# A banded-attention and two-MLP kernel on one core: q and k come transposed, values and weights in blocks, masks from memory

## The chip, the core and the metric

The kernel runs on one core of one Trainium2 chip. Five engines work side by side: PE (matrix products, with its own weight loads), DVE (elementwise work and reductions), ACT (activation functions and copies), POOL (elementwise work; it also issues some transfers) and SP, which here only issues transfers between memory and the chip. Each engine takes its instructions strictly in their written order and waits on semaphores. The metric is the device time of one execution in microseconds, as the median of three runs. Work that the host does before the launch, such as a new layout of the inputs, is not in it.

## What is computed

```python
# q, k, v: (4, 8, 576, 64); heads 0-3 see a plain window, heads 4-7 a dilated one
scores = scale * np.matmul(q, k.transpose(0, 1, 3, 2))
mask_plain = (rel >= 0) & (rel < 32)
mask_dil = (rel >= 0) & (rel < 128) & (rel % 4 == 0)
scores = np.where(masks, scores, -1e9)
attn = softmax(scores); x = attn @ v            # then x: (2304, 512)
h = np.maximum(np.maximum(x @ w1, x @ w2), x @ w3); x = h @ w_out      # d_ff 768
h = x @ w_in                                                          # d_ff 2048
P = a[0] + a[1]*h + a[2]*h**2 + a[3]*h**3
Q = 1 + abs(b[0])*abs(h) + abs(b[1])*h**2
out = (P / (Q + 1e-6)) @ w_out
```

Weights of the MLPs come as 64-bit floats.

## The kernel before, in words

Tokens are cut into 12 chunks of 192 (three to a batch entry), and two chunks make a unit of 384 tokens; there are six units. The attention of a chunk is written as steps, each for group p (the plain heads) and group d (the dilated ones): T transposes the raw rows of k or q on PE (four products with an identity matrix, L265) and copies the result into kTp, kTd (ACT, L274) or into both halves of a block-diagonal qTp, qTd (DVE L278 and ACT L279); S makes the scores (L308 adds the mask as a product for chunks 0 to 3, L317 the score products); MX the row maxima (L334, L337); E the exponentials (L345); SB the division (L355 to L357); X the transpose of the attention weights (L370, with copies L372 or L374); V the product with v (L390, L396); VE the split of the result into two parts x1h and x1l (L411, L412).

The order of this work is written by hand. START lists what comes before the first MLP: chunks 0 and 1, some loads, the first steps of the weight conversion, and W:n, n products of zeros that keep PE busy (L663). UNIT0 and UNIT list the steps of the next unit's two chunks, row by row beside the product groups of the running unit's first MLP. Within this, a scheduler places each instruction on its engine, and it may pull a step of unit 1 up into the end of START.

The weights of the first MLP (18 pieces for the three maxout matrices, 6 for the output matrix) are loaded as 64-bit words and converted on chip. Per piece: an ACT step (L480), three DVE steps on integers (L490, L493, L496), a copy on ACT (L510) and a subtraction on POOL (L518). The three products of every MLP term (L535 to L537) use the two parts. The 32 pieces of the second MLP are converted beside units 1 to 4 and come back from memory later.

The stages in time are: START (up to the first product of L535), unit 0 with the conversion of the first MLP's weights, units 1 to 5 of the first MLP (units 1 to 4 carry the attention of chunks 4 to 11), and the second MLP.

qTp, qTd, kTp and kTd have one buffer each. The raw q and k rows are loaded in pieces of 96 KB, two to a step, six steps ahead. The masks, the identity matrix and the zeros of qTp and qTd are made on chip by POOL and DVE.

Of the kernel before, what the change touches and what calls it, by code (L numbers as in the profile page):

```python
# [17 lines left out]
LN2 = 0.6931471805599453  # L18
# [12 lines left out]
START = """  # L31
# [8 lines left out]
Ta:p,k Ta:p,q Sa:p  # L40
Ta:d,k Ta:d,q MXa:p Ea:p SBa:p
# [7 lines left out]
Va:d Tb:p,k  # L49
VEa:d  # L50
Tb:p,q
Tb:d,k Sb:p
MXb:p Tb:d,q Eb:p
# [11 lines left out]
Ta:p,k  # L65
Ta:p,q Ta:d,k Sa:p Ta:d,q
# [7 lines left out]
Tb:p,k Va:d Tb:p,q  # L74
VEa:d
-
Sb:p Tb:d,k VEa:p
-
-
Tb:d,q MXb:p  # L80
# [10 lines left out]
def kernel(  # L91
    ctx: ExitStack,
    tc: tile.TileContext,
    q: bass.AP,
    k: bass.AP,
    v: bass.AP,
    w1: bass.AP,
    w2: bass.AP,
    w3: bass.AP,
# [8 lines left out]
    B, H, S, D = q.shape  # L108
    NT, DM = out.shape
    FF1 = w1.shape[1]  # L110
    FF2 = w_in2.shape[1]
# [4 lines left out]
    CH = 192  # L116
# [13 lines left out]
    NEG = -1.0e9 / SCALE  # L130
# [9 lines left out]
    T_MM = 2  # L140
    QK = 6
# [43 lines left out]
    # The queries of two heads (or of two residues of a head) stand on the diagonal of one  # L185
    # stationary operand, their keys one above the other in the moving one.
# [4 lines left out]
    qk_seq = [(c, g, nm) for c in range(NCH) for g in ("p", "d") for nm in ("k", "q")]  # L191
    qk_n = [0]

    def load_qk(n):
        while qk_n[0] < min(n, len(qk_seq)):
            c, g, nm = qk_seq[qk_n[0]]
            qk_n[0] += 1
            b, ci = divmod(c, NC)
            src = q if nm == "q" else k
            t0 = CH * ci  # L200
            t = at.tile([2 * M, 2, 4 * D], F32, tag="qk", bufs=QK, name="qk")
            for i in range(2):
                if g == "p":
                    nc.sync.dma_start(
                        out=t[:, i, :].rearrange("p (h d) -> p h d", h=NP),
                        in_=src[b, 0:NP, t0 + 96 * i:t0 + 96 * i + 96, :].rearrange(
                            "h p d -> p h d"))
                else:
                    nc.sync.dma_start(
                        out=t[M * i:M * i + M],  # L210
                        in_=src[b, NP + 2 * i:NP + 2 * i + 2, t0:t0 + CH, :].rearrange(
                            "g (m r) d -> m g (r d)", r=4))
            at_raw[c, g, nm] = t
# [8 lines left out]
    def load_v(c):  # L222
        b, ci = divmod(c, NC)
        vp = at.tile([WP, BP, NP, D], F32, tag="vp", name=f"vp{c}")
        for i in range(BP):
            k0 = key0(ci, i)
            nc.sync.dma_start(
                out=vp[:, i], in_=v[b, 0:NP, k0:k0 + WP, :].rearrange("h p d -> p h d"))
        m0, nm = dil(ci)
# [221 lines left out]
    def cols(w, f):  # L451
        return w[:, 128 * f:128 * f + 128].rearrange("(c p) f -> p c f", p=128)
# [443 lines left out]
```

## Time and profile before

| | us |
|---|---|
| median of 3 runs | 856.75 |
| lowest and highest run | 853.81, 858.59 |
| span of the profiled execution | 857.5 |
| PE busy in that span | 828.7 (97%) |
| DVE busy | 660.1 (77%) |
| ACT busy | 510.7 (60%) |
| POOL busy | 138.6 (16%) |

The span runs from the first to the last instruction of one profiled execution; no other time of that execution is given, and it lies 0.75 us above the median of the runs. Busy shares are means over stages with different limits, and on PE a busy stretch also counts products that run at half the clock.

### The profile page before, as it was taken

What the parts mean: (1) busy time and instruction counts of PE and PEld (TensorE: products, weight loads), DVE (VectorE), ACT (ScalarE), POOL (GpSimd) and SP (SyncE); (2) the same over time, 40 slices, a digit from 0 to 9 for tenths busy, and PEclk for the clock granted to TensorE, in tenths of its full rate; (3) what the DMA queues carried; (4) which work ended last, traced back from release to release, by engine and by line L of the source; (5) the groups of instructions that cost most, each with busy time, mean ns of one, the idle gap of its engine ahead of it and who ended that gap; (6) DMA issues with size and microseconds to landing.
All of it is one profiled execution on the core that took longest, in us unless ns stands there. A gap on an engine that the chain in (4) does not pass through costs nothing.

```text
span 857.5 us, 13838 instructions
## 1 busy us (share of the span) xinstructions
PE 828.7 (97%) x5167; PEld 764.3 (89%) x5167; DVE 660.1 (77%) x1200; ACT 510.7 (60%) x1071; POOL 138.6 (16%) x172
## 2 busy tenths in 40 slices
PE   8997889999999999999998999999999999999997
PEld 6686779999999999999997889999999999999996
DVE  4699956657666756753529899999999999999996
ACT  4575733334333434424548788778778778777775
POOL 3155451120011011104952000000000000000000
PEclk9699999999999999999998999999999999999999
DMA  8675423645646545415740002002002001000100
GB/s 193 167 230 166 142 57 108 176 139 170 180 138 183 166 148 163 137 49 189 223 128 20 1 1 74 1 1 74 1 0 75 1 1 37 2 0 1 38 1 37
DMA packets 77474, 77.57 MB, mean 90 GB/s; under 512 B 37536, under 2 KB 65952, under 8 KB 77408
## 3 DMA queue, kind: packets, MB, share of 16 engines
q1 hardware_dynamic: 72112, 59.66, 24.8%
q0 software_dynamic: 5296, 17.04, 5.4%
q8 instruction: 40, 0.66, 0.3%
q14 instruction: 26, 0.21, 0.1%
HBM read 58.85 MB, written 17.83 MB: 89 GB/s over the span
## 4 chain that ended last, share of the span: by engine, by line
PE 83%; DVE 8%; issue 3%; ACT 3%; DMA 2%; SPq 1%; POOL 0%; ACTq 0%; DVEq 0%
PE mm L537 10%; PE mm L536 10%; PE mm L535 10%; PE acc L832 8%; PE acc L831 8%; PE acc L830 8%; PE h L535 8%; PE h L536 8%; PE h L537 8%; PE sc L317 3%; DVE cvt L496 2%; DVE cvt L493 2%; PE tpp L370 2%; DMA raw<-in_moe_w_in_dram 1%; PE tpq L265 1%
## 5 line engine op out<-in xcount | busy, mean ns | idle before, releaser
L535 PE MATMUL mm<-x1h,w1s 128*128 128x384 f32 x432 | 149.9, 347 | 0.0
L537 PE MATMUL mm<-x1h,w1s 128*128 128x384 f32 x432 | 146.5, 339 | 2.5 <-POOL w1s L518 2.5
L536 PE MATMUL mm<-x1l,w1s 128*128 128x384 f32 x432 | 146.3, 339 | 0.9 <-DVE x1l L412 0.9
L535 PE MATMUL h<-x2h,w2s 128*128 128x384 f32 x384 | 130.9, 341 | 3.8 <-DVE p L791 3.8
L536 PE MATMUL h<-x2l,w2s 128*128 128x384 f32 x384 | 130.5, 340 | 0.0
L537 PE MATMUL h<-x2h,w2s 128*128 128x384 f32 x384 | 130.4, 340 | 0.0
L831 PE MATMUL acc<-w2s,gh 128*128 128x512 f32 x288 | 113.5, 394 | 0.0
L830 PE MATMUL acc<-w2s,gh 128*128 128x512 f32 x288 | 113.2, 393 | 0.0
L832 PE MATMUL acc<-w2s,gl 128*128 128x512 f32 x288 | 110.3, 395 | 0.0
L781 ACT ACTIVATE q<-h 128x384 f32<-128x384 f32 x96 | 47.3, 493 | 80.1 <-PE h L537 79.0
L788 DVE SCALAR_TENSOR_TENSOR q<-q,cs,ab 128x384 f32<-128x384 f32 x96 | 67.7, 705 | 30.3 <-ACT ab L782 30.3
L537 PEld LDWEIGHTS mm<-x1h,w1s 128*128 128x128 f32 x432 | 81.6, 189 | 4.0 <-POOL w1s L518 4.0
L536 PEld LDWEIGHTS mm<-x1l,w1s 128*128 128x128 f32 x432 | 81.9, 190 | 2.2 <-DVE x1l L412 2.2
L535 PEld LDWEIGHTS mm<-x1h,w1s 128*128 128x128 f32 x432 | 81.8, 190 | 0.4
L535 PEld LDWEIGHTS h<-x2h,w2s 128*128 128x128 f32 x384 | 73.0, 190 | 8.2 <-DVE p L791 4.1
L536 PEld LDWEIGHTS h<-x2l,w2s 128*128 128x128 f32 x384 | 73.1, 190 | 3.8
L537 PEld LDWEIGHTS h<-x2h,w2s 128*128 128x128 f32 x384 | 72.9, 190 | 0.3
L554 DVE TENSOR_TENSOR m<-mm,m 128x384 f32<-128x384 f32 x72 | 39.7, 552 | 41.5 <-PE mm L537 23.3
L783 ACT ACTIVATE p<-h,cs 128x384 f32<-128x384 f32 x96 | 65.0, 678 | 0.0
L832 PEld LDWEIGHTS acc<-w2s,gl 128*128 128x128 f32 x288 | 53.9, 188 | 11.8
L797 ACT ACTIVATE r<-q,cs 128x384 f32<-128x384 f32 x96 | 59.6, 621 | 4.8 <-DVE q L788 4.3
L831 PEld LDWEIGHTS acc<-w2s,gh 128*128 128x128 f32 x288 | 54.0, 188 | 9.4
(117 smaller groups left out, 1677.8 us busy)
## 6 DMA issues: line engine op xcount, KB each, us to landing
w1r<-in_moe_w_dram SPq DMA_DIRECT2D x18, 512.0 KB, 6.4
raw<-in_moe_w_in_dram SPq DMA_DIRECT2D x16, 512.0 KB, 4.1
w2d<-cvt POOLq DMA_DIRECT2D x32, 256.0 KB, 3.5
raw<-in_moe_w_out_dram SPq DMA_DIRECT2D x16, 512.0 KB, 3.8
w2r<-w2d SPq DMA_DIRECT2D x32, 256.0 KB, 3.1
qk<-in_k_dram SPq DMA_DIRECT2D x48, 96.0 KB, 3.1
qk<-in_q_dram SPq DMA_DIRECT2D x48, 96.0 KB, 2.7
x2d<-xs POOLq DMA_DIRECT2D x24, 192.0 KB, 2.2
```

Source lines behind the costliest of these rows:

```text
L317: nc.tensor.matmul(scs[n // G][:, n % G, :], lhsT=lq, rhs=rk, start=not pem, stop=not pem or n % G == G - 1)
L535: nc.tensor.matmul(o, lhsT=lh, rhs=rh, start=(i == 0), stop=False)
L536: nc.tensor.matmul(o, lhsT=lh, rhs=rl, start=False, stop=False)
L537: pe_at[0] = nc.tensor.matmul(o, lhsT=ll, rhs=rh, start=False, stop=(i == n - 1))
L554: nc.vector.tensor_tensor(out=t, in0=o, in1=t, op=ALU.max)
L781: nc.scalar.activation(out=s["q"], in_=s["h"], func=AF.Square)
L783: nc.scalar.activation(out=s["p"], in_=s["h"], func=AF.Identity, scale=cs[:, 3:4], bias=cs[:, 2:3])
L788: nc.vector.scalar_tensor_tensor(out=s["q"], in0=s["q"], scalar=cs[:, 5:6], in1=s["ab"], op0=ALU.mult, op1=ALU.add)
L797: nc.scalar.activation(out=s["r"], in_=s["q"], func=AF.Ln, scale=LS, bias=cs[:, 6:7])
L830: nc.tensor.matmul(o, lhsT=gh, rhs=w[:, 0:512], start=(c == 0), stop=False)
L831: nc.tensor.matmul(o, lhsT=gh, rhs=w[:, 512:1024], start=False, stop=False)
L832: nc.tensor.matmul(o, lhsT=gl, rhs=w[:, 0:512], start=False, stop=(c == F2 - 1))
```

## The change

The host lays the inputs out anew. k comes transposed for a whole batch entry (kTp, kTd, two buffers each), q comes transposed and already with its zeros, chunk by chunk (qTp, qTd, two buffers each, twice the bytes of the raw rows), v comes in one block per group and chunk, the weight pieces come with each partition's words in one run, and the identity matrix and both masks come as one tensor, mk. The step T is gone, with its products on PE and its copies on ACT and DVE, and so are the mask building and the two memsets of qTp and qTd. START is written anew, with 29 products W instead of 39 and other places for the loads. The loads of chunk c+2's q stand behind the scores of chunk c.

```diff
 START = """
 W:7
-T0:p,k W:1 T0:p,q v:0 W:2 T0:d,k T0:d,q L:3 W:1 S0:p MX0:p E0:p S0:d MX0:d W:3
-T1:p,k T1:p,q SB0:p T1:d,k T1:d,q E0:d X0:p,0,1 W:2 X0:p,1,1 W:1 S1:p MX1:p V0:p SB0:d abs VE0:p b0 b1 E1:p S1:d abs X0:d,0,1 W:2 MX1:d X0:d,1,1 W:4 V0:d E1:d W:2 SB1:p b2 VE0:d hi abs lo v:1 L:3
-X1:p,0 W:2 SB1:d X1:p,1 bits W:4 V1:p hi W:2 VE1:p lo b0 b1
-X1:d,0 W:2 X1:d,1 W:4 V1:d VE1:d b2 hi lo abs
+S0:p v:0 L:3 S0:d MX0:p E0:p MX0:d S1:p W:2
+SB0:p E0:d X0:p,0,1 X0:p,1,1 W:1 MX1:p V0:p SB0:d abs VE0:p b0 b1 E1:p S1:d abs X0:d,0,1 W:2 MX1:d X0:d,1,1 W:3 V0:d E1:d W:2 SB1:p b2 VE0:d hi abs lo v:1 L:3
+X1:p,0 W:2 SB1:d X1:p,1 bits W:3 V1:p hi W:2 VE1:p lo b0 b1
+X1:d,0 W:2 X1:d,1 W:3 V1:d VE1:d b2 hi lo abs
 """
...
-        def T(g, nm):
-            raw = at_raw.pop((c, g, nm))
...
-                nc.tensor.transpose(tp[:, o:o + 96], rows, ident[:96, :96])
...
-                nc.scalar.activation(out=dst, in_=src, func=AF.Copy)
-                return
...
-            nc.vector.tensor_copy(dst[0:64, :, 0:w], src[0:64])
-            nc.scalar.activation(out=dst[64:128, :, w:2 * w], in_=src[64:128], func=AF.Copy)
...
+            load_q(c + QA, g)
+            if g == "d" and ci == 0 and b + 1 < B:
+                load_k(b + 1)
...
+        mk = const.tile([128, 128 + BP * WP + 2 * WD], F32, name="mk")
+        ident = mk[:, 0:128]
...
+        load_k(0, 0)
+        load_q(0, "p")
+        nc.sync.dma_start(out=mk, in_=masks)
+        kTd0 = at_k[0][1]
+        nc.sync.dma_start(out=kTd0.rearrange("p n m -> p (n m)"), in_=kd_in[0])
+        load_q(0, "d")
+        load_q(1, "p")
+        load_k(0, 1)
+        load_q(1, "d")
```

UNIT0 and UNIT lose their T words and keep the places of the other steps.

In the queue of SP the first loads are now few and large. Before, from the start of the program (qk are raw rows, co the coefficients, vp and vd the values of chunk 0):

```order
L204 DMA qk<-in_k_dram 96x4x64 x2
L204 DMA qk<-in_q_dram 96x4x64 x2
L209 DMA qk<-in_k_dram 48x2x256 x2
L209 DMA qk<-in_q_dram 48x2x256 x2
L204 DMA qk<-in_k_dram 96x4x64 x2
L204 DMA qk<-in_q_dram 96x4x64 x2
L605 DMA co<-in_moe_a_dram 128x4
L606 DMA co<-in_moe_b_dram 128x2
```

And with the change, from the same place:

```order
L205 DMA kTp_139<-in_kp_dram 128x2x192
L217 DMA qTp_142<-in_qp_dram 128x768
L578 DMA mk<-in_masks_dram 128x576
L580 DMA kTd_140<-in_kd_dram 128x1152
L220 DMA qTd_146<-in_qd_dram 128x768
L217 DMA qTp_148<-in_qp_dram 128x768
L208 DMA kTp_139<-in_kp_dram 128x2x384
L220 DMA qTd_151<-in_qd_dram 128x768
L586 DMA co<-in_a_dram 128x4
L587 DMA co<-in_b_dram 128x2
L217 DMA qTp_184<-in_qp_dram 128x768
```

Eight loads of 192 to 576 KB stand where loads of 96 KB stood; the coefficients moved behind them, and the first part of q for chunk 2 (qTp_184) follows at once, behind a wait for the scores of chunk 0.

On PE, the place in START from the second X of chunk 0's group p to V of the same group. Before (sc the scores, mP the mask, pv the product with v; the scores here are those of chunk 1):

```order
L370 MATMUL tpp<-ident,sb 96x128 x3
L663 LDWEIGHTS warm
L663 MATMUL warmth<-warm 128x512
L308 LDWEIGHTS ident_168
L308 MATMUL sc<-mP_224,ident_168 128x288
L308 LDWEIGHTS ident_168
L308 MATMUL sc<-mP_224,ident_168 128x288
L317 MATMUL sc<-kTp_238,qTp 128x96 x6
L390 MATMUL pv<-pt,vp_263 64x64 x12
```

And with the change:

```order
L280 LDWEIGHTS ident_156
L280 MATMUL sc<-mP_158,ident_156 128x288
L280 LDWEIGHTS ident_156
L280 MATMUL sc<-mP_158,ident_156 128x288
L345 MATMUL tpp<-mk,sb 96x128 x3
L611 LDWEIGHTS warm
L611 MATMUL warmth<-warm 128x512
L289 MATMUL sc<-kTp_139,qTp_184 128x96 x6
L365 MATMUL pv<-pt,vp_189 64x64 x12
```

The scores of chunk 1 have moved up ahead of X, and the scores between X and V are now those of chunk 2, which stood in unit 0 before; their mask products stand ahead of X and wait for a score bank that E of chunk 0's group d still reads.

On DVE, the end of START from the division of chunk 1's group d to the last split x1l. Before:

```order
L357 TENSOR_TENSOR sb<-sb,sm 96x640
L490 TENSOR_SCALAR cvt<-cvt 128x512
L493 SCALAR_TENSOR_TENSOR cvt<-w1r_1_293,cvt 128x512
L496 SCALAR_TENSOR_TENSOR cvt<-w1r_1_293,cvt 128x512
L412 TENSOR_TENSOR x1l_241<-pv,x1h_240 128x2x192
L490 TENSOR_SCALAR cvt<-cvt 128x512
L493 SCALAR_TENSOR_TENSOR cvt<-w1r_2_295,cvt 128x512
L412 TENSOR_TENSOR x1l_241<-pv,x1h_240 128x2x4x48
```

And with the change:

```order
L332 TENSOR_TENSOR sb<-sb,sm 96x640
L459 TENSOR_SCALAR cvt<-cvt 128x512
L462 SCALAR_TENSOR_TENSOR cvt<-w1r_1_195,cvt 128x512
L465 SCALAR_TENSOR_TENSOR cvt<-w1r_1_195,cvt 128x512
L309 TENSOR_REDUCE mx<-sc 96x4
L330 TENSOR_SCALAR sm<-sm 128x6
L331 RECIPROCAL sm<-sm 128x6
L332 TENSOR_TENSOR sb<-sb,sm 128x576
L387 TENSOR_TENSOR x1l_173<-pv,x1h_172 128x2x192
L459 TENSOR_SCALAR cvt<-cvt 128x512
L462 SCALAR_TENSOR_TENSOR cvt<-w1r_2_197,cvt 128x512
L387 TENSOR_TENSOR x1l_173<-pv,x1h_172 128x2x4x48
```

The division of chunk 2's group p and half the maxima of its group d have moved from unit 0 into START; the maxima of its group p did so further up, and its exponentials on ACT with them.

## Rows read from the trace of the kernel before

**Rows 1.** Windows: length; PE, PEld, DVE, ACT, POOL busy (count); clock, DMA share, GB/s.
```profile
41.20:119.00 77.80, 65.69 (x477) 58.84 (x477) 74.08 (x109) 47.81 (x130) 39.75 (x27) 0.96 0.55 161
121.00:430.00 309.00, 306.66 (x2314) 299.59 (x2315) 188.59 (x346) 123.00 (x236) 63.84 (x79) 1.00 0.51 153
430.00:857.50 427.50, 419.30 (x2092) 379.97 (x2090) 375.49 (x691) 318.13 (x626) 24.74 (x31) 0.99 0.07 24
```

**Rows 2.** Chain of waits in START: start us, us, what.
```profile
7.33 3.31 DMA co<-in_moe_b_dram
...
11.93 1.12 ACT sb L345 x7
...
14.44 0.77 DVE sb L357
...
24.98 2.09 ACT sb L345 x13
...
30.38 1.71 PE warmth L663 x4
...
40.25 0.62 PE mm L535
```

**Rows 3.** Timeline of PE in START: start us, us, instruction, idle before it.
```profile
20.22 0.92 PE L390 MATMUL pv<-pt,vp 96*64 96x64 f32 x24
21.38 1.51 PE L317 MATMUL sc<-kTd,qTd 128*96 128x80 f32 x16
...
29.68 0.69 PE L370 MATMUL tpp<-ident,sb 128*96 128x128 f32 x3 [1.88 <-ACT pt L374]
```

**Rows 4.** Windows of one microsecond in START, columns as in rows 1.
```profile
14.00:15.00 1.00, 0.55 (x4) 0.36 (x4) 0.92 (x3) 0.95 (x3) 0.00 (x0) 1.00 1.35 111
...
20.00:21.00 1.00, 1.00 (x27) 0.90 (x26) 0.64 (x3) 0.00 (x0) 0.00 (x0) 1.00 1.14 356
...
30.00:31.00 1.00, 1.00 (x4) 0.41 (x3) 0.93 (x3) 0.49 (x1) 0.05 (x1) 0.50 1.10 314
```

**Rows 5.** Instructions that write the raw q and k tiles, to 60 us.
```profile
DMA to landing us min/median/max: 2.1/2.9/8.6
```

**Rows 6.** Timeline of DVE in unit 0: start us, us, instruction, idle before it.
```profile
41.20 0.86 DVE L412 TENSOR_TENSOR x1l<-pv,x1h 128x384 fp32r<-128x384 f32 x1 [5.17 <-ACT x1h L411]
...
46.73 0.55 DVE L278 COPY qTp<-tpq 64x384 f32<-64x384 f32 x1
...
49.49 0.81 DVE L334 TENSOR_REDUCE mx<-sc 128x3 f32<-128x288 f32 x2
...
55.81 0.99 DVE L357 TENSOR_TENSOR sb<-sb,sm 128x576 f32<-128x576 f32 x1
...
73.38 1.77 DVE L493 SCALAR_TENSOR_TENSOR cvt<-w1r,cvt 128x512 int32<-128x512 int32 x1
...
82.82 0.55 DVE L554 TENSOR_TENSOR m<-mm,m 128x384 f32<-128x384 f32 x1
```

**Rows 7.** Timeline of POOL in unit 0.
```profile
47.41 1.60 POOL L518 TENSOR_TENSOR w1s<-cvt,w1s 128x512 fp32r<-128x512 f32 x1 [2.76 <-ACT w1s L510]
...
73.06 1.53 POOL L518 TENSOR_TENSOR w1s<-cvt,w1s 128x512 fp32r<-128x512 f32 x1 [1.29 <-ACT w1s L510]
...
82.97 1.29 POOL L518 TENSOR_TENSOR w1s<-cvt,w1s 128x512 fp32r<-128x512 f32 x1 [1.29 <-ACT w1s L510]
```

**Rows 8.** Windows of DVE's copies of L278 alone: length, busy (count), clock, DMA.
```profile
41.20:121.00 79.80, 2.17 (x4) 0.96 0.53 157
```

**Rows 9.** Windows of T alone (tile tpq): PE, PEld, DVE, ACT.
```profile
121.00:430.00 309.00, 16.77 (x128) 13.77 (x128) 8.68 (x16) 15.60 (x32) 1.00 0.51 153
```

**Rows 10.** Chain of waits in unit 1 around one T.
```profile
129.65 0.33 PE tpq L265 x4
129.98 0.20 PE mm L535
130.18 0.17 PE mm L536
```

More of the change, by code (lines that the diff above doesn't have):

```diff
@@ L6 @@
 from concourse._compat import with_exitstack
-from concourse.masks import make_identity
 F32 = mybir.dt.float32
@@ L48 @@
 -
-Va:d Tb:p,k
+Va:d
 VEa:d
-Tb:p,q
-Tb:d,k Sb:p
-MXb:p Tb:d,q Eb:p
+-
+Sb:p
+MXb:p Eb:p
 Sb:d MXb:d SBb:p Eb:d Xb:p,0
@@ L64 @@
 UNIT = """
-Ta:p,k
-Ta:p,q Ta:d,k Sa:p Ta:d,q
+-
+Sa:p
 -
@@ L73 @@
 Xa:d,1 Va:p Xa:d,0
-Tb:p,k Va:d Tb:p,q
+Va:d
 VEa:d
 -
-Sb:p Tb:d,k VEa:p
+Sb:p VEa:p
 -
 -
-Tb:d,q MXb:p
+MXb:p
 -
@@ L93 @@
     tc: tile.TileContext,
[L94 to L99, printed above, removed]
+    masks: bass.AP,
+    kp_in: bass.AP,
+    kd_in: bass.AP,
+    qp_in: bass.AP,
+    qd_in: bass.AP,
+    vp_in: bass.AP,
+    vd_in: bass.AP,
+    w123: bass.AP,
     w_out1: bass.AP,
@@ L107 @@
     nc = tc.nc
[L108 removed]
+    B, H, S, D = BATCH, HEADS, SEQ, DIM
     NT, DM = out.shape
[L110 to L111 removed]
+    FF1 = w_out1.shape[0]
+    FF2 = w_out2.shape[0]
     NP = H // 2
@@ L189, with load_k, load_q @@
     x1 = {}
[L191 to L213, printed above, removed]
+    def load_k(b, part=None):
+        if b not in at_k:
+            at_k[b] = (
+                at.tile([128, 2, S], F32, tag="kTp", bufs=2, name=f"kTp{b}"),
+                at.tile([128, 8, S // 4], F32, tag="kTd", bufs=2, name=f"kTd{b}"),
+            )
+        kTp, kTd = at_k[b]
+        src = kp_in[b].rearrange("p (a t) -> p a t", a=2)
+        if part is None:
+            nc.sync.dma_start(out=kTp, in_=src)
+        elif part == 0:
+            nc.sync.dma_start(out=kTp[:, :, 0:CH], in_=src[:, :, 0:CH])
+            return
+        else:
+            nc.sync.dma_start(out=kTp[:, :, CH:S], in_=src[:, :, CH:S])
+            return
+        nc.sync.dma_start(out=kTd.rearrange("p n m -> p (n m)"), in_=kd_in[b])
+    def load_q(c, g):
+        if c >= NCH:
+            return
+        if g == "p":
+            t = at.tile([128, 2 * BP, 2 * QP], F32, tag="qTp", bufs=QA, name=f"qTp{c}")
+            nc.sync.dma_start(out=t.rearrange("p n w -> p (n w)"), in_=qp_in[c])
+        else:
+            t = at.tile([128, 8, 2 * M], F32, tag="qTd", bufs=QA, name=f"qTd{c}")
+            nc.sync.dma_start(out=t.rearrange("p n w -> p (n w)"), in_=qd_in[c])
+        at_raw[c, g] = t
     def key0(ci, blk):
@@ L222, in load_v @@
     def load_v(c):
-        b, ci = divmod(c, NC)
+        ci = c % NC
         vp = at.tile([WP, BP, NP, D], F32, tag="vp", name=f"vp{c}")
[L225 to L229, printed above, removed]
+        nc.sync.dma_start(out=vp.rearrange("p i h d -> p (i h d)"), in_=vp_in[c])
+        nm = dil(ci)[1]
         vd = at.tile([WD, NP, 4 * D], F32, tag="vd", name=f"vd{c}")
-        nc.sync.dma_start(
-            out=vd[:nm],
-            in_=v[b, NP:H, 4 * m0:4 * (m0 + nm), :].rearrange("h (m r) d -> m h (r d)", r=4))
+        nc.sync.dma_start(out=vd[:nm].rearrange("p h e -> p (h e)"), in_=vd_in[c, 0:nm, :])
         at_raw[c, "v"] = (vp, vd)
@@ L252, in attn_pieces @@
         pts = {}
[L254 to L279 removed]
         def SC(g):
             plain = g == "p"
+            qT = at_raw.pop((c, g))
             U, Q, W = (2 * BP, 2 * QP, WP) if plain else (8, 2 * M, nmk)
@@ L313, in SC @@
                     k0 = key0(ci, blk)
-                    lq, rk = qTp[:, n, :], kTp[:, i, k0:k0 + WP]
+                    lq, rk = qT[:, n, :], kTp[:, i, k0:k0 + WP]
                 else:
-                    lq, rk = qTd[:, n, :], kTd[:, n, m0:m0 + nmk]
+                    lq, rk = qT[:, n, :], kTd[:, n, m0:m0 + nmk]
                 nc.tensor.matmul(scs[n // G][:, n % G, :], lhsT=lq, rhs=rk,
                                  start=not pem, stop=not pem or n % G == G - 1)
+            load_q(c + QA, g)
+            if g == "d" and ci == 0 and b + 1 < B:
+                load_k(b + 1)
             sb = at.tile([Q, U, WP if plain else WD], F32, tag="s" + g, bufs=SBB, name="sb")
@@ L463, in cv_load @@
             _, side, c = order2[f]
-            src, ascols = (w_in2, True) if side == 0 else (w_out2, False)
+            src = w_in2[c] if side == 0 else w_out2[128 * c:128 * c + 128, :]
         else:
-            src, ascols, c = (w_out1, False, f) if kind == "wo1" else ((w1, w2, w3)[j], True, f)
-        if ascols:
-            ld = nc.sync.dma_start(out=raw.rearrange("p (c f) -> p c f", c=KC), in_=cols(src, c))
-        else:
-            ld = nc.sync.dma_start(out=raw, in_=src[128 * c:128 * c + 128, :])
+            src = w_out1[128 * f:128 * f + 128, :] if kind == "wo1" else w123[3 * f + j]
+        ld = nc.sync.dma_start(out=raw, in_=src)
         if kind == "w2":
@@ L881 @@
     arrays, args = {}, []
-    for name in _INS:
-        a = _np.ascontiguousarray(inputs[name])
+    for name, a in _laid_out(inputs).items():
+        a = _np.ascontiguousarray(a)
         if a.dtype == _np.float64:
```

140 lines of the change are left out of this document (72 added, 68 removed).

## Prediction

> **What bounds the kernel now.** I read the windows by stage first, since the page's busy shares mix stages. In units 1 to 5 PE is busy 306.66 of 309.0 us, and in the second MLP 419.30 of 427.5 [rows 1]: there PE is the bound, and DVE and ACT have a third of their time or more to spare in units 1 to 5 (188.59 and 123.00 of 309). In unit 0 it is DVE, busy 74.08 of 77.80 us while PE has 12.1 us of holes: the conversion of the first MLP's weights goes through it. START is neither; it is a chain, which I read from the chain of waits: a load, maxima, exponentials, division, X, and so on, up to the first product of the MLP at 40.25 [rows 2]. DVE stands 5.17 us until the last x1h of START and is full from 41.20 on [rows 6], so whatever START gives up is handed on to unit 0 in full. Each stage is costed by its own limit, and the second MLP, which the change does not touch, at nothing.
>
> **Units 1 to 4: T leaves PE.** All 128 transposes there (32 steps T of four) lie in a stage that PE fills [rows 9]. One step takes 0.33 us in the chain, and the product behind it 0.20 instead of 0.17 [rows 10]; so 0.36, and 32 of them make 11.5 us. This is the lower bound. The upper one adds all of the stage's idle time of PE, 309.0 - 306.66 = 2.3, if it all came from waits around T: 13.8. I take 12.0, since most of that idle time has other causes that stay. The 16 copies on DVE (8.68 us) and 32 on ACT (15.60) [rows 9] that go as well lie beside PE's work and count for nothing.
>
> **START.** T goes here too, but T is mostly beside the chain, so I walk the chain instead. Loads: a load of 96 KB takes at least 2.1 us from issue to landing [rows 5], and the best second in START moved 356 GB/s [rows 4]; I use 350. A load then lands at about 2.6 us plus all bytes ahead of it and its own over 350: mk (885 thousand bytes from the start) at 5.1, qTd of chunk 0 at 7.9, the rest of kTp at 10.2, the coefficients at some 11.5. The chain: two small casts of the masks, the scores of group p from 5.4 to about 7.8 (a like step takes 1.51 at full clock [rows 3], twice that at half, and I take 2.4 with its mask product), maxima to 8.4, exponentials and division 3.3 us as before (11.93 to 15.21 [rows 2]), so 11.7. Behind them on ACT stand group d's exponentials, an estimated 2.3 us (13 of chunk 1's 16 pieces take 2.09 [rows 2], and these are narrower), to 12.8. Their scores wait for loads that land by 7.9 and are done in time. PE comes free for X only behind the scores of chunk 1, which wait for kTp until 10.2; they are done at 11.6 and cost nothing, because the second X stands behind the mask products of chunk 2, which wait for those exponentials until 12.8. Second X to 13.6, a W, the scores of chunk 2 (1.4, as the 1.51 of a like step [rows 3]), and V of chunk 0 starts at 15.2. Before it started at 20.22 [rows 3]: 5.0 us earlier. From there to E of chunk 1's group d (24.98) and the second X of chunk 1 (29.68) [rows 2, 3] the steps are the same in the same order on the engine that ends last at each, so the 5.0 is kept. The 3.31 us that the maxima stood behind the coefficients' load [rows 2] is gone, as those now land before DVE comes to them.
>
> From the second X of chunk 1 to the first MLP product took 40.25 - 29.68 = 10.6 us, PE full but at a granted clock of 0.50, which is 1.2 GHz [rows 4]; it fell there after PE had stood 1.88 us [rows 3]. That wait is ACT's and stays, so I take half clock again. New in this stretch: half the scores of chunk 2's group d, 1.5 at half clock (half of 1.51, doubled), and a mask product of 0.3. Gone: two W of 0.43 each (1.71 for four [rows 2]). Net 1.0 later. START ends **4.0 us** earlier. Bounds: nothing, if the loads or the clock take it all; 8.8, with the tail at full clock (first rival).
>
> SP's queue now holds waits for PE: q of chunk 2 waits for the scores of chunk 0, and behind it stand the values of chunk 0 and the first weights. At 350 GB/s the eight loads ahead keep the queue busy until 11, past that wait (7.8), so nothing is late. The values of chunk 1 have 8.16 million bytes up to and with them: landing at 25.9, wanted by V of chunk 1 at about 28.5 (24.8 for its second X, then the four steps below).
>
> **Unit 0.** Gone from DVE: four copies of L278, 2.17 us busy [rows 8], some 1.9 as they overlap their neighbours a little. Moved into START, where DVE has room: two maxima of 0.81 together, the division of 0.99 [rows 6], half of the group d maxima (about 0.4) and three tiny steps (0.3): 2.5. Together **4.4 us**. Bounds: nothing if another limit stands right behind (third rival); 7.4 with the stage's own idle time, of which DVE has 3.7 (77.80 - 74.08 [rows 1]), nearly all gone too. The eight copies on ACT for T go unpriced: ACT is busy 47.81 of 77.80 and seldom last.
>
> A rule bears on this term. POOL's subtraction and DVE's integer steps slow one another: a step of L493 that starts inside a subtraction takes 1.77 us [rows 6, 7]. A step that reads its result from PE's bank does not: L554 takes 0.55 right beside one [rows 6, 7]. The copies of L278 are of this second kind, so a copy that ran under a subtraction would have cost nothing. The first one ran at 46.73, when POOL was idle until 47.41 [rows 6, 7], and I count all four as paid for.
> The Trainium skill, page "SBUF — State Buffer", section "Who interferes with whom", says why: DVE and POOL share a port pair that is locked for a whole instruction, and a DVE step with at most one SBUF input stays out of it; by this rule, if the lock were what binds unit 0, neither the copies nor the maxima would give anything, which is the third rival. The trace agrees with the lock, and leaves open whether it binds.
>
> **At nothing.** Mask building on POOL and the memsets: they ended before START's first maxima, and the load of mk, which takes their place, is in the chain above. If mk came later, START would slip by as much. Values in fewer loads and weights in longer runs: conversions wait for DVE, not for loads; if a load were late, unit 0 would wait for it.
>
> **Sum.** 12.0 + 4.0 + 4.4 = 20.4 us. 857.5 - 20.4 = 837.1 for a profiled span; the median of the runs lies 0.75 below the span, so **836.4**.
>
> **Rivals.** *The clock stays up in START's tail.* For it: PE's work ahead of the tail is denser now, with T and ten W gone and the scores of two more groups in their place. Against it: PE's 1.88 us stand comes back. The tail of 11.6 would take about 6.8 (half, and a us for copies that do not shrink): 4.8 less, 831.6.
>
> *START gains nothing.* The loads ahead of the first scores are several times as big, and some small ones already took 8.6 us to land [rows 5]. If mk lands at 9.1 instead of 5.1, the chain starts 4.0 late and the gain is 16.4: 840.4. Against it: nothing else is under way when the first three loads start.
>
> *Unit 0 is bound by the shared work of DVE and POOL, not by DVE's own list.* POOL is busy 39.75 of 77.80 [rows 1], DVE's stretched steps hide under it. Then 4.4 falls away: 840.8.
>
> *PE is not the bound once T is gone.* Then the 12.0 would turn into waits in units 1 to 4: 848.4. Against it, DVE has 120 us free there.
>
> *Slower: START starves.* START must now load 8.16 million bytes before V of chunk 1. In one second the engines of the queue were over-full (1.35) and moved only 111 GB/s [rows 4]. At that rate the values of chunk 1 land at 76 us, not 25.9, V of chunk 1 is some 48 us late, and the time is 836.4 + 48 = 884. It decides at about 177 GB/s, where the values land at 48.7 and the 20.4 are eaten up. Against it: other seconds moved 314 and 356 GB/s [rows 4], and the loads of that second came in runs of 256 bytes to 1 KB, where now a run has about 3 KB.
>
> **Chances.** My forecast 0.54, clock up 0.16, START without gain 0.12, the shared limit 0.10, PE not the bound 0.04, starving 0.04. The range runs from the upper bounds of the two larger terms with the third as taken, 856.75 - (13.8 + 8.8 + 4.4) = 829.8, to the lower bound of the first alone, 856.75 - 11.5 = 845.3, so 829 to 846; outside lie the last two rivals and a sum of good luck. Within 0.5% (4.3 us, about what a measurement of this kernel can tell) lies part of the starving case only: 0.03; slower 0.03; faster 0.94.
>
> **What would show it.** Right: no L265; first MLP product near 36; DVE full from 37 to about 111; units 1 to 5 shorter by 12 with PE still over 99% busy; the second MLP's length unchanged. Wrong: DVE idle early in START before the first maxima (loads), a granted clock of 1.00 through START's tail, unit 0 as long as before, or PE waiting for q loads in units 1 to 4.

## The result, and the profile after

The changed kernel takes 842.36 us (median of 4 runs, 840.17 to 843.29) against 856.62 for the kernel before, a ratio of 0.9828 with a 95% interval of 0.9801 to 0.9855. It is faster by 14.3 us; 20.4 were forecast, and 836.4 lies 6 us under the measured time.

The profiled execution has a span of 838.4 us and took 840.17, the shortest of its four (the other spans are 841.5, 840.5 and 840.6). Its counterpart of before is a long one: in the runs here the time is the span and some 1.8, so that the span of 857.5 stands for some 859.3, above the longest timed run. The two traces therefore differ by 19.1 us, 4.8 more than the medians. In the page of after, the busy times that answer to the table of before:

```profile
PE 808.7 (96%) x4965; PEld 750.4 (89%) x4965; DVE 646.2 (77%) x1172; ACT 488.5 (58%) x1023; POOL 133.8 (16%) x145
```

I cut both traces at the same events: the first product of the first MLP, the issue of the last result of units 0, 4 and 5, and the end. The windows (columns as in [rows 1]) of the kernel before:

```profile
40.18:128.44 88.26, 75.78 (x530) 68.34 (x529) 74.08 (x109) 51.16 (x136) 42.81 (x31) 0.96 0.50 149
128.44:391.01 262.57, 260.50 (x2023) 253.94 (x2024) 168.67 (x320) 99.67 (x190) 32.68 (x54) 1.00 0.49 144
391.01:443.86 52.85, 52.61 (x338) 52.06 (x333) 21.74 (x28) 25.38 (x51) 34.34 (x27) 1.00 0.62 200
443.86:857.50 413.64, 405.44 (x2012) 366.17 (x2010) 373.67 (x689) 314.23 (x619) 19.77 (x25) 0.99 0.06 21
```

and of the changed one:

```profile
39.38:125.58 86.20, 73.52 (x477) 68.41 (x475) 66.98 (x98) 46.28 (x116) 43.97 (x31) 0.88 0.47 166
125.58:374.56 248.98, 248.25 (x1895) 243.23 (x1896) 162.65 (x304) 84.32 (x158) 32.52 (x55) 1.00 0.50 163
374.56:427.34 52.78, 52.54 (x337) 52.04 (x333) 22.27 (x28) 25.21 (x51) 34.06 (x28) 1.00 0.51 160
427.34:838.40 411.06, 403.25 (x2012) 364.15 (x2010) 373.50 (x689) 314.31 (x619) 19.80 (x25) 0.99 0.06 21
```

START ends 0.8 us earlier (40.18 to 39.38). Unit 0 is 2.1 shorter (88.26 to 86.20), although DVE is busy 7.1 less in it. Units 1 to 4 are 13.6 shorter (262.57 to 248.98), with PE idle 0.7 us where 2.1 were idle before. Unit 5 is as long as it was. The second MLP, which the change does not touch, is 2.6 shorter; an experiment below shows where it varies. A second trace of the kernel before, whose only edit lies in START (before_w_tail, below), has 88.08 us for unit 0, 261.31 for units 1 to 4 with PE idle for 0.9, and 412.46 for the second MLP. Against that trace units 1 to 4 are 12.3 us shorter and the second MLP 1.4.

START after, in PE's timeline (start, length, instruction, and in brackets the idle time and its releaser):

```profile
7.82 0.66 PE L280 MATMUL sc<-mP,ident 128*128 128x288 bf16 x2 [3.33 <-POOL ident L589]
8.28 2.71 PE L289 MATMUL sc<-kTp,qTp 128*128 128x96 f32 x12
...
11.10 1.67 PE L289 MATMUL sc<-kTd,qTd 128*96 128x48 f32 x16
...
12.86 1.47 PE L289 MATMUL sc<-kTp,qTp 128*128 128x96 f32 x12
...
18.30 0.92 PE L365 MATMUL pv<-pt,vp 96*64 96x64 f32 x24
...
27.70 0.53 PE L345 MATMUL tpp<-mk,sb 128*96 128x128 f32 x3 [1.87 <-ACT pt L349]
...
29.77 0.42 PE L280 MATMUL sc<-mD,ident 96*96 96x320 bf16 x1 [0.69 <-ACT sb L320]
...
39.38 0.69 PE L504 MATMUL mm<-x1h,w1s 128*128 128x384 f32 x1
```

PE stands 3.33 us until POOL has cast the identity matrix out of mk. The load of mk was issued at 2.08 and landed at 7.28. The first score step takes 2.71 us, the third 1.47. V of chunk 0 starts at 18.30, and from the second X of chunk 1 to the MLP pass 11.7 us. In the trace of an experiment whose START is not edited (bank_pv, below) the same rows read:

```profile
8.18 0.66 PE L280 MATMUL sc<-mP,ident 128*128 128x288 bf16 x2 [3.69 <-POOL ident L589]
...
14.42 2.71 PE L289 MATMUL sc<-kTp,qTp 128*128 128x96 f32 x12
...
21.08 0.92 PE L365 MATMUL pv<-pt,vp 96*64 96x64 f32 x24
...
30.47 0.53 PE L345 MATMUL tpp<-mk,sb 128*96 128x128 f32 x3 [1.87 <-ACT pt L349]
...
42.15 0.69 PE L504 MATMUL mm<-x1h,w1s 128*128 128x384 f32 x1
```

Here the score steps are still slow at 14.42, V of chunk 0 starts 2.8 us later, and START ends at 42.15. The q of chunk 2 landed at 15.0 in this trace, before the scores that need it (19.67), so that load is not what holds PE here. All four traces of experiments with an unedited START (bank_pv, t_pe, u0_dve, b_early) end it late, at 41.77 to 42.15. The three executions of the changed kernel that were not profiled are also 2.1 to 3.1 us longer than the profiled one. So the profiled execution was most likely a lucky one: START of the changed kernel commonly ends 1.6 to 2.0 us *later* than before. The kernel before repeats its START: a second trace with the same first half (before_w_tail, below) has the second X of chunk 1 at 29.74, against 29.68 [rows 3].

In unit 0, PE waits for the last part of the output weights, and works off what is left. Before (the lines at 121.04 and 127.40, the first product of unit 1) and after:

```profile
121.04 0.80 PE L537 MATMUL mm<-hh,wo1s 128*128 128x384 f32 x3 [0.37 <-POOL wo1s L518]
...
127.40 0.33 PE L535 MATMUL mm<-x1h,w1s 128*128 128x384 f32 x1
```

```profile
90.63 0.32 PE L280 MATMUL sc<-mD,ident 96*96 96x192 bf16 x1 [5.07 <-ACT sb L320]
...
111.88 0.69 PE L506 MATMUL mm<-hh,wo1s 128*128 128x384 f32 x1 [1.03 <-POOL wo1s L487]
...
124.54 0.33 PE L504 MATMUL mm<-x1h,w1s 128*128 128x384 f32 x1
```

The last wait ends 80.9 us after START before (121.04 - 40.18) and 72.5 after (111.88 - 39.38), so the conversions are 8.4 us quicker. But behind it PE needs 6.4 us before and 12.7 after: of the 72 output products it had issued 36 by then before, and 14 after. It came late to them because it had stood 5.07 us for a score bank that the exponentials of chunk 3 still read, and the products behind 111.88 ran at a granted clock of 0.50 until 117 (0.32 us each instead of 0.17).

### The profile page after: what moved, and what is told of

It reads as the page before. It is cut to its first block, busy times and chain, and to the rows that moved or that the text cites. A ratio compares the mean times of both kernels' runs of the same rounds, so it can differ in the third digit from the quotient of the medians.

```text
span 838.4 us, 13171 instructions
## 1 busy us (share of the span) xinstructions
PE 808.7 (96%) x4965; PEld 750.4 (89%) x4965; DVE 646.2 (77%) x1172; ACT 488.5 (58%) x1023; POOL 133.8 (16%) x145
## 4 chain that ended last, share of the span: by engine, by line
PE 86%; issue 5%; POOL 3%; ACT 3%; DVE 3%; DMA 1%; SPq 0%; POOLq 0%; ACTq 0%; DVEq 0%
PE mm L505 10%; PE mm L506 10%; PE mm L504 10%; PE acc L780 8%; PE acc L778 8%; PE acc L779 8%; PE h L505 8%; PE h L504 8%; PE h L506 8%; PE sc L289 3%; POOL w1s L487 2%; PE tpp L345 2%; PE pv L371 1%; PE pv L365 1%; POOL wo1s L487 1%
## 5 line engine op out<-in xcount | busy, mean ns | idle before, releaser
L505 PEld LDWEIGHTS h<-x2l,w2s 128*128 128x128 f32 x384 | 72.5, 189 | 3.8
```

The source lines that it names most:

```text
L505: nc.tensor.matmul(o, lhsT=lh, rhs=rl, start=False, stop=False)
```

## The experiments

Each ratio is to the kernel before, on the same chip. Lines in the profile rows are those of the kernel run.

**Masks built on chip again (masks_on_chip).**

```diff
-        nc.sync.dma_start(out=mk, in_=masks)
...
+        for i, off in ((0, 0), (1, 32)):
+            band(mP32[0:64, i], off, 0)
...
```

> The changed kernel, but identity and masks are built on chip by POOL as before, and the load mk is gone. Theory: START gave back its gain because the first scores stood until mk's load had landed (7.28 us; PE idle 3.33 us until the casts). With the masks ready at about 5.2 us (POOL's end in the kernel before) the first scores start at 5.2 to 6.2 instead of 7.82 and the first product of the MLP comes 1.5 to 2.5 us before 39.4; the time falls by 1 to 2.5 us. Rival: kTp and qTp themselves (576 KB) land only at about 7 us; then the scores start no more than 0.5 us earlier and the time stays.

847.76 us, ratio 0.9889 (0.9861 to 0.9918): 5 us slower than the changed kernel, and START ends at 47.05. PE's timeline:

```profile
5.31 0.64 PE L281 MATMUL sc<-mP,ident 128*128 128x288 bf16 x2 [0.75 <-POOL mP L614]
...
10.34 2.77 PE L290 MATMUL sc<-kTd,qTd 128*96 128x48 f32 x16 [1.57 <-DMA qTd<-in_qd_dram]
...
19.96 0.40 PE L281 MATMUL sc<-mP,ident 128*128 128x288 bf16 x1 [3.01 <-ACT sb L321]
```

The first scores do start 2.5 us earlier, at 5.31, so mk's load was what they waited for. But the time does not follow: the scores of group d now stand for their own load, and in SP's queue two weight loads moved ahead of chunk 2's q (presumably since the scheduler plans them by the earlier scores); that q was issued at 10.29 and landed 11.1 us later. The experiment changed two things and so does not price the masks. It shows that START after hangs on several loads, one behind another, not on mk alone.

**Chunk 2's group d held back (hold_s2d).**

```diff
+                    if (c, g) == (2, "d"):
+                        tc.add_manual_dep(mm.ins, pe_at[0].ins.name, PACE, reason="not in START")
```

> The changed kernel, with the scores of chunk 2's group d kept out of START by a dependency, so that they run in unit 0. Theory: in START's tail they cost PE 0.69 us of waiting for ACT's exponentials of chunk 2's group p, 1.4 us of half of the scores at half clock and 0.5 us of mask products, so the first product of the MLP comes 2.2 to 2.6 us earlier (36.8 to 37.2 instead of 39.4), and the time falls by 1 to 2.5 us. Rival: the tail's end is set by the chain of copies on ACT and DVE, not by PE; then less than 0.7 us earlier, and unit 0 takes back the work: no gain or up to 1 us slower.

841.09 us, ratio 0.9821 (0.9802 to 0.9841). PE's timeline:

```profile
29.51 0.53 PE L347 MATMUL tpp<-mk,sb 128*96 128x128 f32 x3 [1.87 <-ACT pt L351]
...
38.91 0.69 PE L506 MATMUL mm<-x1h,w1s 128*128 128x384 f32 x1
```

From the second X to the MLP pass 9.4 us instead of 11.7: 2.3 less, as the theory says (I had priced these scores at 1.8 together, without the wait of 0.69). The MLP does not start at 36.8 to 37.2, since the second X itself came at 29.51 in this trace. The ratio is lower than that of the changed kernel by 0.6 us, which is less than the two intervals can tell, so a gain in the time is not shown.

**The banks of chunk 3 (bank_pv).**

```diff
-    SC_AT = {(0, "p"): "pv", (1, "p"): "mm", (1, "d"): "pv"}
+    SC_AT = {(0, "p"): "pv", (1, "p"): "mm", (1, "d"): "pv", (3, "d"): "pv"}
```

> The changed kernel, with the scores of chunk 3's group d in the two banks of V (pv) in place of the score banks that the exponentials of its group p still read. The order on PE stays the same. Theory: PE's waits of 5.07 and 0.65 us in unit 0 go, PE comes to the output products 5 us earlier, and the clock has no cause to fall there; unit 1 starts 4 to 6 us earlier (118.5 to 120.5 instead of 124.5) and the time falls by 4 to 6 us. Rival: the weights of the next products are not converted yet, so PE waits for POOL's subtractions in place of the bank and unit 1 starts less than 1 us earlier; the wait for the bank hid it.

839.91 us, ratio 0.9806 (0.9788 to 0.9825). Unit 0 has 84.28 us, 1.9 less, not 4 to 6. The stand of 5.07 is gone, and a longer one has come, in PE's timeline:

```profile
99.08 0.85 PE L345 MATMUL tpp<-mk,sb 128*96 128x128 f32 x3 [6.39 <-DVE sb L332]
```

PE now stands for DVE's division of the same chunk. The theory was half right: the bank was only the first link of a chain (scores, maxima, exponentials, division), and the next link is DVE's. PE has 14 output products behind it at its last wait, as in the changed kernel; what was gained comes from the clock, which stayed at 1.00 behind that wait (10.4 us to the first product of unit 1 instead of 12.7).

**T's products alone (t_pe).**

```diff
+        def T(g, nm):
+            tp = tp_p.tile([128, TU], F32, tag="tp", name="tpq")
+            for i in range(4):
+                nc.tensor.transpose(tp[:, 96 * i:96 * i + 96], ident[:96, :], ident[:96, :96])
```

> The changed kernel, with 32 times four transposes of the identity matrix added on PE at the old places of T in units 1 to 4; nobody reads the result, and there are no copies. Theory: T cost its time on PE alone, 0.36 us for each step: 11.5 us longer, and up to 13.6 (the shortening of units 1 to 4 in the two traces) if the waits around T are PE's own too. Rival: a part of the gain came from the copies and waits around T; then clearly less than 10 us longer.

851.97 us, ratio 0.9948 (0.9931 to 0.9965); between the ratios lie 10.3 us (0.0120 of 856.6). Units 1 to 4 take 260.17 us, 11.2 more than 248.98, in the windows of the added tile:

```profile
128.14:388.31 260.17, 16.76 (x128) 13.77 (x128) 1.00 0.48 157
```

The 128 transposes keep PE busy as long as those of before (16.77 [rows 9]). 11.2 over 32 steps is 0.35 each, the 0.36 of the prediction. What is left, 2.4 of 13.6 us or 1.1 of 12.3 by the second trace of before, would belong to the waits and copies around T; this experiment shows it only as a rest.

**More W ahead of the scores (w14).**

```diff
-W:7
+W:14
```

> The changed kernel with 14 products W in place of 7 ahead of the first scores. So far the same START ended at 39.4, 42.2 and 41.9 us in three traces: in the two late ones every product up to 17 us took its half-speed time (score steps of group p 2.71 us instead of 1.47), in the early one up to 10.8 us. Theory: that is because PE stands 3.3 to 3.7 us for mk's load; with PE busy until then, the scores of chunk 0 and 1 take 1.5 us a step, V of chunk 0 starts at 17 to 18 us and the MLP at 38 to 39; the time falls by 1.5 to 3.5 us. Rival: the loads set these times, and the slow products hide behind them; then V of chunk 0 starts at 20 us or later and the time stays.

841.39 us, ratio 0.982 (0.9783 to 0.9857): no change, and START ends at 42.02. PE's timeline:

```profile
8.26 0.66 PE L280 MATMUL sc<-mP,ident 128*128 128x288 bf16 x2 [0.79 <-POOL ident L589]
...
14.50 2.71 PE L289 MATMUL sc<-kTp,qTp 128*128 128x96 f32 x12
```

With a stand of only 0.79 us the steps are as slow as with one of 3.7. V of chunk 0 starts at 20.93 and the time stays, as the rival has it; but PE did stand until mk came, so the theory is not refuted either.

**W in START's tail (w_tail).**

```diff
-X1:p,0 W:2 SB1:d X1:p,1 bits
+X1:p,0 W:10 SB1:d X1:p,1 bits
```

> The changed kernel with 10 products W in place of 2 between the two X of chunk 1's group p, where PE stands 1.87 us for ACT's copy. Theory: this stand is what the granted clock falls to 0.50 after; with PE busy it stays at 1.00, and the stretch from the second X to the first product of the MLP takes 7 to 8 us instead of 11.7, so the time falls by 3 to 4.5 us. Rival: the clock falls all the same (PE waits a little at many other places); then the stretch stays at 11.5 to 12 us and the time within 1 us.

837.45 us (837.12 to 837.99), ratio 0.9782 (0.9753 to 0.9812). PE's timeline:

```profile
30.43 0.53 PE L345 MATMUL tpp<-mk,sb 128*96 128x128 f32 x3 [0.18 <-ACT pt L349]
...
38.08 0.45 PE L504 MATMUL mm<-x1h,w1s 128*128 128x384 f32 x1
```

The stretch takes 7.65 us instead of 11.7, at a granted clock of 1.00 from 30 to 38 where it was 0.50. Eight products of zeros, laid into a stand that was there anyway, give back 4.0 us of this stretch. The time falls by 3.9 (0.9828 less 0.9782, of 856.6), but not by START alone: in this trace the second MLP, too, is 2.3 us shorter than in that of the changed kernel (408.80). For the clock in the tail the theory holds.

**DVE's copies of T in unit 0 (u0_dve).** Four times, PE makes four transposes that nobody uses, and DVE reads them from PE's bank.

```diff
+            nc.vector.tensor_reduce(out=scr, in_=tp[0:64].rearrange("p (n w) -> p n w", n=4),
+                                    axis=AX.X, op=ALU.max)
```

> The changed kernel with four steps of T for q put back into unit 0: four transposes of the identity matrix on PE each, and one DVE step that reads the bank (a maximum over 64 x 384 numbers, some 0.5 us); nobody reads the result. Theory of the prediction: DVE's list sets the end of unit 0, so unit 0 gets 1.9 to 2.2 us longer, and the time too. Rival: unit 0's end is set by PE, which falls behind at the wait for chunk 3's exponentials; then unit 0 gets longer by less than 0.7 us. Second rival: all that DVE does later makes that wait longer as well; then 2.5 us or more.

840.31 us, ratio 0.981 (0.9779 to 0.9841). The four steps, in the view of their line (shortest, median, longest in ns):

```profile
L257 DVE TENSOR_REDUCE scr<-tpq x4: 537/537/549, 46.1 to 94.6; 64x4 f32<-64x384 f32 x4
```

They are as long as the four copies that the change removed (2.16 us together, 2.17 in [rows 8]). DVE's last conversion ends only 0.6 us later after START (71.9 instead of 71.3), and unit 0 takes 86.56 us instead of 86.20, 0.4 more. DVE is busy 1.3 us more in the stage (68.29 instead of 66.98), not 2.16, so its other steps became 0.8 us shorter in sum; its 64 integer steps take 51.8 us instead of 55.4. Steps of this kind cost 0.4 to 0.6 us at these places, as the first rival had it, and not 1.9. What the copies themselves cost is not shown by it: all four steps ran beside a subtraction of POOL here (at 46.11, 50.13, 87.24 and 94.62), while in the trace before only one of the four copies did (at 86.40). The time says nothing on this, since the second MLP is 3.3 us shorter in this trace (407.7) than in that of the changed kernel.

**Chunk 3 three rows earlier (b_early).**

```diff
-Sb:p
-MXb:p Eb:p
-Sb:d MXb:d SBb:p Eb:d Xb:p,0
+Va:d Sb:p
+VEa:d MXb:p Eb:p
+Sb:d MXb:d SBb:p Eb:d Xb:p,0
...
```

> The changed kernel with the steps of chunk 3 three rows earlier in unit 0's list. Keeping chunk 3's scores in other banks only moved PE's stand of 5.7 us to the next step (6.4 us for DVE's division). Theory: PE comes too late to the output products because chunk 3's chain of scores, maxima, exponentials and division stands ahead of them on PE and is held up by DVE, which is full; with the chain earlier, PE has weight products left to do behind it, the stand shrinks below 2 us, more than half of the output products are done when the last weights are converted, and unit 0 gets 3 to 5 us shorter. Rival: DVE is full all the time, so an earlier chain pushes the conversions back, and PE waits as long for weights; unit 0 stays within 1 us.

842.23 us, ratio 0.9837 (0.9807 to 0.9867). Unit 0 has 85.49 us, 0.7 less: the rival. PE's stand for the bank is 4.45 us, not below 2. PE has 26 output products behind it at its last wait instead of 14, but that wait ends 76.4 us after START (118.14 - 41.77) instead of 72.5: an earlier chunk 3 pushes the conversions back.

**19 W and the tail (w19_tail).**

```diff
-W:7
+W:19
...
-X1:p,0 W:2 SB1:d X1:p,1 bits
+X1:p,0 W:10 SB1:d X1:p,1 bits
```

> The changed kernel with 19 products W ahead of the first scores and 10 in the tail of START. With 14 ahead, PE still stood 0.79 us before the first scores and every product stayed slow until 17.8 us (a score step of group p 2.71 us); in the kernel before, PE had no stand until 12.3 us and the same steps took 1.47 us from 7.8 us on. Theory: any stand while PE is still slow starts the slow stretch anew, so with PE busy until mk has landed the first scores take 1.5 us, V of chunk 0 starts at 17 to 18 us instead of 21, the MLP at 34 to 35.5 instead of 38.1, and the time falls by some 3 us below the 837.5 of the tail alone. Rival: the slow stretch ends at about 17 us whatever PE does; then V of chunk 0 stays at 21 to 22 us and the time within 1 us of the tail alone.

836.42 us (836.31 to 836.65), ratio 0.9761 (0.9741 to 0.9782). PE's timeline:

```profile
8.72 1.47 PE L289 MATMUL sc<-kTp,qTp 128*128 128x96 f32 x12
...
12.03 1.55 PE L289 MATMUL sc<-kTp,qTp 128*128 128x96 f32 x12
...
17.61 2.77 PE L289 MATMUL sc<-kTp,qTp 128*128 128x96 f32 x12 [1.35 <-DMA qTp<-in_qp_dram]
20.31 1.55 PE L365 MATMUL pv<-pt,vp 96*64 96x64 f32 x24
```

Now the first scores take 1.47 us, as in the kernel before, so the rival that the slow stretch lasts until 17 us whatever PE does falls. The products are slow from the first W on; here the W start 0.43 us apart up to 7.27 and 0.22 apart from 7.61, and PE does not stand before the scores. But V of chunk 0 starts at 20.31, not at 17 to 18: behind the fast scores PE stands 1.35 us for the q of chunk 2, which took 7.3 us to land, and is slow again. START is now held by that load, as the rival of w14 has it, and ends later than in w_tail:

```profile
39.33 0.44 PE L504 MATMUL mm<-x1h,w1s 128*128 128x384 f32 x1
```

So the 1.0 us between the medians of the two (3 were expected) is not START's: in these traces the second MLP is 1.3 us shorter than in w_tail, and unit 0 is 0.8 shorter.

**Five edits together (best).** W:19, W:10 in the tail, and the edits of hold_s2d, bank_pv and b_early.

> The changed kernel with five edits together: 19 W ahead of the first scores, 10 in START's tail, chunk 2's group d kept out of START, chunk 3's steps three rows earlier, and the scores of its group d in the banks of V. Theory: the edits of START add up (MLP from 32.5 to 34 us instead of 42), and the two of unit 0 as well, because the one takes away the stand for the bank and the other gives PE work behind the division (unit 0 82 to 84 us instead of 86.2): 829 to 833 us. Rival: unit 0 is set by DVE and POOL's conversions and takes back what START gives, since DVE starts earlier but has chunk 2's group d to do as well; unit 0 gets 87 us or longer, and the time stays at 834 or more.

836.74 us (834.86 to 838.09), ratio 0.977 (0.9743 to 0.9797). PE's timeline:

```profile
17.06 0.92 PE L367 MATMUL pv<-pt,vp 96*64 96x64 f32 x24
...
34.81 0.44 PE L506 MATMUL mm<-x1h,w1s 128*128 128x384 f32 x1
```

Here the q of chunk 2 came in time, V of chunk 0 started at 17.06 and the MLP at 34.81, 7 us before the common 42. Unit 0 has 83.8 us, as expected, and the MLP starts 0.8 us behind the 34 expected. The first MLP ends 6.2 us before that of w19_tail (420.92 and 427.10), yet the median is no better, and the 829 to 833 expected were missed: in this trace the second MLP takes 412.2 us (833.1 - 420.92), in that of w19_tail 407.5. Neither theory had that; what the second MLP stands for is told in the last section, and the last run tests it. (Its other executions are up to 3.2 us longer than the profiled one.)

**The tail in the kernel before (before_w_tail).** The edit of w_tail, in the kernel before.

> The kernel before, with 10 W in place of 2 between the two X of chunk 1's group p. It has the same stand of 1.88 us there, and a granted clock of 0.50 behind it. Theory: the lost clock in START's tail is no matter of the change; the stretch from the second X to the first product of the MLP falls from 10.6 to 6 to 7 us and the time by 3 to 4.5 us. Rival: in the kernel before the clock falls for another reason or the tail waits for ACT and DVE; less than 1 us. Its trace is also a second look at the kernel before up to 28 us of START, which is not edited: V of chunk 0 at 20 to 20.5 us if the first trace was a common one, and 1 to 3 us later if it was a lucky one.

853.34 us (7 runs), ratio 0.9958 (0.9942 to 0.9974). PE's timeline:

```profile
29.74 0.53 PE L370 MATMUL tpp<-ident,sb 128*96 128x128 f32 x3 [0.17 <-ACT pt L374]
...
36.91 0.44 PE L535 MATMUL mm<-x1h,w1s 128*128 128x384 f32 x1
```

7.2 us instead of 10.5 (40.18 - 29.68), a little more than the 6 to 7 expected: the lost clock was there before the change, and costs START 3.3 us. The time falls by 3.6 us (by the ratio).

**The second MLP's subtractions on DVE (best_w2_dve).**

```diff
-        nc.gpsimd.tensor_sub(t[:, 512:1024], r, t[:, 0:512].bitcast(F32))
+        nc.vector.tensor_sub(t[:, 512:1024], r, t[:, 0:512].bitcast(F32))
```

> The five edits together, and the 32 subtractions that split the second MLP's weights on DVE instead of POOL. The second MLP is not touched by the change, but its start differs from trace to trace: while POOL runs nine subtractions on end (11.2 us), one DVE step of 0.6 us takes 9.0 us, PE stands 3.8 us for it and the clock falls behind that; in two traces POOL had gaps, the step took 6.6 us, PE stood 1.4 us and the second MLP was 3.4 us shorter. Theory: with DVE doing the subtractions there is nothing to be locked out by; the stand goes, the stretch from unit 5's last result to the end takes 405 to 408 us instead of 412, and the time falls to 830 to 833 us with runs closer together than the 834.9 to 838.1 of the five edits. Rival: the subtractions wait for loads, and in DVE's strict order the maxima and splits of unit 5 wait behind them; PE stands there instead, and the time stays at 836 or more.

831.0 us (5 runs, 828.96 to 831.74), ratio 0.969 (0.9674 to 0.9706): the best of all, 11 us under the changed kernel. Its windows, cut as above:

```profile
37.52:121.68 84.16, 71.44 (x487) 66.08 (x485) 68.72 (x100) 45.92 (x116) 44.40 (x31) 0.92 0.47 170
121.68:370.82 249.14, 248.34 (x1895) 243.24 (x1896) 163.02 (x304) 84.47 (x158) 32.52 (x55) 1.00 0.50 163
370.82:423.55 52.73, 52.49 (x337) 52.12 (x333) 28.40 (x51) 25.61 (x51) 2.16 (x5) 1.00 0.48 160
423.55:828.90 405.35, 401.39 (x2012) 362.62 (x2010) 370.52 (x698) 313.79 (x619) 8.54 (x16) 1.00 0.06 21
```

The second MLP takes 405.35 us, 5.7 less than in the trace of the changed kernel, at a clock of 1.00 and without the stand at its start. START ends at 37.52 here, not at 34.81, so it still varies; the runs are hardly closer together (828.96 to 831.74) than those of best.

## Why the prediction came out as it did

**Units 1 to 4** were right in mechanism and nearly in size: 13.6 for 12.0 by the first trace of the kernel before, just inside the upper bound of 13.8, and 12.3 by the second. Whether "most of that idle time has other causes that stay" is open: PE's idle time is 0.7 us after, where the two traces of before have 2.1 and 0.9. No wait for q loads came in, and PE is still the bound; t_pe shows that PE's own time for T is the price.

**START** failed: 4.0 forecast, 0.8 in the profiled execution, some -1.7 (40.18 less 41.9) commonly, which is beyond the lower bound of nothing. Two steps of the walk failed, both ahead of V of chunk 0. The loads were taken to land one behind another, mk at 5.1; it landed at 7.28. The likely reason, which no run here tests, is that five more loads were issued by 5 us and shared the engines with it: up to 7 us the trace has moved 1.26 million bytes (86, 339 and 205 GB/s over two us each from 1 us on), where the three loads up to mk have 0.885. And only the first scores were priced at half speed: the scores of chunk 1 were to be "done at 11.6", while in the common execution three score steps of 2.5 us and their mask products lie in the chain until 17. w19_tail and best bear out the slow steps: with PE kept busy until mk was there they took 1.5 us, and when the q of chunk 2 came in time as well, V of chunk 0 started at 17.06. From V of chunk 0 to the second X of chunk 1 the walk held: 9.40 us in the profiled execution and 9.39 in bank_pv, where [rows 3] has 9.46. The tail went as predicted in kind (half clock again, the hoisted scores in it), with 1.2 lost for 1.0 (11.7 instead of 10.5). The first rival, a tail at full clock, was priced at 4.8; it did not happen by itself, and w_tail measured 4.0 for it.

**Unit 0** gave 2.1 for 4.4, by another balance than the one written down. DVE's part was too small: the last weights came 8.4 us sooner. DVE is busy 7.1 less, and 2.5 of that are its 64 integer steps, which take 55.4 us instead of 57.8 and were not in the sum. That term was to be handed on in full, because DVE bound the stage; the step that failed is that the end of unit 0 is DVE's last conversion *and* the output products that PE has left then. The window of [rows 1] hid them: it stops at 119.00, where DVE is done (74.08 us in 109 steps, as many as up to 128.44 in the window above), and unit 1 begins at 127.40. What PE had left grew from 6.4 to 12.7 us, as it was still held by chunk 3's chain. bank_pv and b_early each moved the wait elsewhere. Steps like the copies, priced at 1.9, cost 0.4 to 0.6 in u0_dve, where they ran beside POOL's subtractions. The Trainium skill, page "SBUF — State Buffer", section "Who interferes with whom", has it that a DVE step with at most one SBUF input stays out of the pair that DVE shares with POOL. The trace agrees: beside POOL's subtractions all four took 0.54 to 0.55 us.

**The sum.** Commonly: -1.7 + 2.1 + 13.6 = 14.0, and 14.3 were measured. By the second trace of the kernel before it is -1.7 + 1.9 + 12.3, with 0.4 in unit 5 and 1.4 in the second MLP, which is 14.3 too; how the total is shared between the stages is known to about a us. Against the forecast, 5.7 us are START, 2.3 unit 0, and 1.6 came back in units 1 to 4. So the time lies inside the stated range with two of the three terms off, START and unit 0, and nearer to the rivals at 840.4 and 840.8 than to the forecast. START gained nothing, as the first of these had it, but mk came at 7.28 and not at 9.1, and no rival had the slow steps behind it. Unit 0 did not go by the other: the weights did come sooner. The 0.75 us between span and median was the difference of two executions and an offset, and cancels, as 857.5 - 0.75 is the median. The rival of starving loads was rightly rejected: from 0 to 36 us the trace after moves 289 GB/s, above the turning point of 177, and V of chunk 1 waited for its values by at most 0.4 us in the traces here.

**Left open:** what sets the order in which the first loads land; why the slow stretch ended at 11 us in the profiled execution and near 17 in others, since in hold_s2d the first scores started earlier still (7.56) and a score step at 13.80 took 2.71; and in unit 0 how to end the stand for chunk 3, which is 5.7 us even in best.

## What to carry to other kernels

When several large loads replace many small ones, do not count on the one that the first step needs to land as if it were alone: look in the trace. In these traces a tensor engine that stood for it at the start of the program did its next steps at half speed as well (2.71 us instead of 1.47), so the wait was paid twice. A stage that is bound by an engine which feeds the tensor engine does not end when that engine is done: count what the tensor engine has left at that moment, since work moved or waits added ahead of it can eat the whole gain. A known stand of the tensor engine can be filled with useless products: eight of them cost nothing here and gave back 4 us of the stretch behind them.

## What the hardware showed that was not expected

*One DVE step can be locked out by a row of POOL steps.* At the start of the second MLP POOL splits nine weight pieces on end. In the timeline of the changed kernel:

```profile
427.89 11.24 POOL L552 TENSOR_TENSOR w2s<-w2r,w2s 128x512 fp32r<-128x512 f32 x9
...
430.53 9.03 DVE L736 SCALAR_TENSOR_TENSOR q<-q,cs,ab 128x384 f32<-128x384 f32 x1 [14.04 <-ACT ab L730]
...
440.72 0.44 PE L504 MATMUL h<-x2h,w2s 128*128 128x384 f32 x1 [3.80 <-DVE p L739]
```

A DVE step that otherwise takes 0.61 us takes 9.03, until POOL's row ends; PE stands 3.80 for what follows it, and then has a granted clock of 0.57 from 441 to 445. In w19_tail POOL's nine steps take 12.01 us, and the same rows are

```profile
430.29 6.58 DVE L736 SCALAR_TENSOR_TENSOR q<-q,cs,ab 128x384 f32<-128x384 f32 x1 [14.04 <-ACT ab L730]
...
438.04 0.45 PE L504 MATMUL h<-x2h,w2s 128*128 128x384 f32 x1 [1.36 <-DVE p L739]
```

with a second MLP of 407.5 us in place of 411.1. The kernel before has the long form too (POOL's row 11.21 us, DVE's step 9.00), and so have all the traces here in which POOL does this work but w_tail, w19_tail and u0_dve. Between these traces it goes with some 3.5 us in a stage that none of their edits touches, so it may also part executions of one kernel; since both first traces have the long form, the 2.6 us between their second MLPs (1.4 by the second trace of before) stay open. The Trainium skill, page "SBUF — State Buffer", section "Who interferes with whom", has the lock held for a whole instruction; here one step of DVE was held over several instructions of POOL, and the measurement decides. best_w2_dve took POOL's steps away, and the stand with them.

*PE's slow stretch in START does not show in the granted clock.* From 1 to 17 us the rows of t_pe show 1.00 all along. Yet 14 W took 6.16 us in w14, 0.43 each after the first, as long as the four W at a granted clock of 0.50 (1.71 [rows 2]), where ten took 2.32 later in w_tail. Only the lengths of the products tell it.
